# Polysketch attention into a squared-ReLU MLP: key and query projections in 64-row tiles, gated products on GpSimd, and a new order of the work

## The chip, the cores and the metric

The kernel runs on one core of a Trainium2 chip. The metric is the time of one execution on the device in microseconds. Of the kernel before there are three timed runs, 113.18, 113.51 and 114.02 us, with a median of 113.51, and one execution that was taken by the profiler, 113.43 us. The engines are called by the names of the profile: PE (matrix products), ACT (ScalarE), DVE (VectorE), POOL (GpSimd) and SP, which here only issues transfers.

## The reference

There are four batches of four heads, 1088 tokens each, head width 32, and two sketch matrices S1 and S2 of 8 x 32.

```python
def phi(x):
    a = np.einsum('rd,bhsd->bhsr', S1, x)
    b = np.einsum('rd,bhsd->bhsr', S2, x)
    return np.einsum('bhsi,bhsj->bhsij', a, b).reshape(*x.shape[:-1], r * r)
q_p, k_p = phi(q), phi(k)
kv = np.einsum('bhsf,bhsd->bhfd', k_p, v)
z = np.sum(k_p, axis=2)
num = np.einsum('bhsf,bhfd->bhsd', q_p, kv)
den = np.einsum('bhsf,bhf->bhs', q_p, z)[..., None] + 1e-06
attn = num / den
x = attn.transpose(0, 2, 1, 3).reshape(4352, 128)
h = np.maximum(x @ w_in, 0.0)          # w_in 128 x 2048
out = (h * h) @ w_out                  # w_out 2048 x 128
```

So every token of every head gets 64 features, the products of 8 values a with 8 values b. kv and z are sums over all tokens of a batch, so nothing of a batch's queries can be finished before all of its keys have been seen.

## The kernel before

**The plan.** The kernel does not issue its work as it describes it. Each step is recorded with `op(...)` (line 44): its engine or engines to choose from, an assumed duration, and the tiles that it reads and writes. `ORDER` (line 122) is a list of the numbers of all steps; `Plan.run` (line 67) walks through it, gives each PSUM tile a buffer, and the instructions are issued in that order, each on its engine. `ALT` names the steps that take the second of their engines. Each engine works through its own instructions in this order. A step whose `port` is true is one that the plan does not let run on DVE and GpSimd at the same time.

**PSUM.** There are two buffers `h` of two banks each and four buffers `t` of one bank each.

**Keys.** Batch 0 has code of its own (`k1`, line 357). For batches 1 to 3 `k_stage` (line 454) transposes the keys on DVE (`kT`, line 457), projects them (K1, line 463, eight matmuls of 128 rows by 32 columns into one t buffer, four for a and four for b), transposes the result to `kab` (line 468), does the same for the remainder of 64 tokens (K1r, line 476, and `kabr`, line 481), and multiplies a by b to `kp` on GpSimd (lines 488 and 495). `z_stage` sums for the denominator (z, line 406; Wc, line 415), `kv_stage` accumulates kv (line 426), and KV4T (line 448) transposes it.

**Queries.** For batches 1 to 3 `compact` (line 673) projects the transposed queries to a and b (qpr, line 686, eight matmuls into one t buffer) and to c, the denominator's part (qpc, four more). DVE transposes these (`qab`, line 690; `qc`, line 692), multiplies c by a into `t9` (ac, line 694), sums it (den), takes the reciprocal, scales a by it (`qaq`, a', line 698), and makes the products of a' and b in two halves (`qo`, line 706), each of which it transposes to `qd` (line 643). All the factors lie in SBUF. `x_turned` (line 648) multiplies qd by kv on 16 places of the array at once (line 662, rows and columns in groups of 32) into one h and two t buffers; it is called xe1, xe2 and xe3 for the batches 1 to 3, x1 and x8 for what remains. Its results are copied to `xT`.

**The MLP.** `f_stage` (line 740) takes 512 tokens (chunks 1 to 7) or 256 (0a, 0b and 8). F1 (line 764) writes two matmuls of 512 columns into an h buffer, ACT takes the ReLU into `r` (line 775), DVE or in places ACT squares it into `g` (line 784), and F2 (lines 791 and 794) accumulates into a t buffer, whose result goes through `osb` to the output by transfers that SP issues. F1 and the ReLU take turns on the two h buffers.

**Loads.** The keys and queries of batch 0 and most of its values come in by SP's queue. All later ones, `w_in` and `w_out` are issued by GpSimd, between its products. `load_v` (line 278) makes four transfers for a batch.

Of the kernel before, what the change touches and what calls it, by code (L numbers as in the profile page):

```python
# [17 lines left out]
class Op:  # L18
    __slots__ = ("eng", "fn", "name", "preds", "dma", "allocs", "uses", "n", "start", "end", "pri", "port")
# [11 lines left out]
class Plan:  # L31
# [12 lines left out]
    def op(self, eng, dur, fn, reads=(), writes=(), name="", dma=None, pri=None, port=False):  # L44
# [18 lines left out]
        o.n, o.start = len(self.ops), None  # L63
# [3 lines left out]
    def run(self, slots, t0=0.7):  # L67
        free = {e: t0 for e in ("PE", "ACT", "DVE", "POOL", "SP")}
        port = 0.0
# [9 lines left out]
        for o in self.order:  # L79
# [9 lines left out]
            if o.port and e in ("DVE", "POOL"):  # L89
                s = max(s, port)  # L90
            if o.dma is not None:
                l = lane["SW" if e == "POOL" else "HW"]
                s = max(s, l[-8] if len(l) > 7 else 0.0)
            o.eng, o.start, o.end = [(e, d)], s, s + d
            free[e] = s + d - (OVER.get(e, 0.0) if o.dma is None else 0.0)
            if o.port and e in ("DVE", "POOL"):
                port = s + d
# [16 lines left out]
TOK = ("0a", "0b", "7", "8")  # L114
SQA = ("0a", "0b", "1")
KPP = 5
FIRST4 = True
# [29 lines left out]
]  # L147
ALT = {67: 1, 91: 1, 110: 1, 127: 1, 131: 1, 137: 1, 155: 1, 161: 1, 318: 1, 387: 1, 423: 1, 425: 1}
# [3 lines left out]
def kernel(  # L152
# [39 lines left out]
    Wab = T("Wab", [128, 2, H, r])  # L192
    Wt = [T(f"Wt{b}", [128, 3, 32]) for b in range(B)]
# [13 lines left out]
    kab = ring("kab", 2, [128, 2, 8, 32])  # L207
    kabr = ring("kabr", 2, [64, 2, 32])
# [9 lines left out]
    qab = ring("qab", 1, [128, 2, 256])  # L218
    qc = ring("qc", 1, [128, 256])
# [7 lines left out]
    rr = ring("r", 3, [128, 4, 512], BF16)  # L227
    gg = ring("g", 3, [128, 4, 512], BF16)
    osb = ring("osb", 2, [128, 512])
    P = Plan()  # L230
    op, tmp = P.op, P.tmp

    def pb(t):
        return tb[t.i] if t.kind == "t" else hb[t.i][:, 0]
# [712 lines left out]
```

## Time and profile before

| what | value |
|---|---|
| median of three runs | 113.51 us |
| profiled execution | 113.43 us, its span 111.7 us, granted clock 0.99 |
| first F1 matmul | at 17.14 us |
| last F2 matmul ends | at 107.1 us |
| ACT, ReLU of 1024 columns | x67, 65.8 us, 1027 ns each |
| DVE, square of 2048 columns | x30, 35.9 us, 1201 ns each |
| DVE, qo of 1024 columns | x6, 9.9 us, 1651 ns each |
| GpSimd, kp of 512 columns | x12, 14.7 us, 1236 ns each |
| PE, F1 with 512 columns | x112, 389 ns each |

The profile shows one execution. Its span runs from the first instruction of the program to the last; the time of the execution is 1.7 us longer. Durations of single instructions include some overlap with the next one on the same engine, so that a piece of the chain, which goes from start to start, is shorter than the instruction's duration. A float32 matmul appears as two records.

### The profile page before, as it was taken

How to read it: one execution, taken by the hardware profiler on the slowest of the kernel's cores; microseconds unless marked ns; L12 is line 12 of the kernel's file. 1: busy time of each engine (PE TensorE's matmuls, PEld its weight loads, DVE VectorE, ACT ScalarE, POOL GpSimd, SP SyncE). 2: the span in 40 equal slices, each digit the busy share in tenths (PEclk: the TensorE clock that was granted, in tenths of full speed). 3: DMA queues.
4: the chain of work that ended last, by engine and by line, in shares of the span. 5: the costliest groups of instructions: out<-in, count | busy, mean ns of one | idle time of the engine just before them, and what ended most of it. 6: DMA issues, size and time to landing. Idle time of an engine off the chain costs nothing.

```text
span 111.7 us, 3330 instructions
## 1 busy us (share of the span) xinstructions
PE 102.7 (92%) x1388; PEld 63.4 (57%) x1388; DVE 92.7 (83%) x134; ACT 83.8 (75%) x113; POOL 32.9 (29%) x50
## 2 busy tenths in 40 slices
PE   7999999999997999979999999999799989999930
PEld 5677856767773645534455455445355545578910
DVE  2569699998999999999989997979877998675810
ACT  3240276999999479994789698969869998999910
POOL 7269147969999910720000000000000000000000
PEclk9999999999999999999999999999999999999995
DMA  1999999821880712000210220033003203222022
GB/s 38 286 262 244 211 387 260 230 79 61 257 246 3 214 55 61 16 6 12 35 18 6 41 47 6 10 61 58 6 0 59 35 5 56 39 47 50 6 70 71
DMA packets 18479, 10.20 MB, mean 91 GB/s; under 512 B 13936, under 2 KB 16928, under 8 KB 18464
## 3 DMA queue, kind: packets, MB, share of 16 engines
q0 software_dynamic: 1824, 6.11, 19.5%
q1 hardware_dynamic: 16384, 3.67, 15.8%
q10 hardware_dynamic: 256, 0.20, 0.8%
q8 instruction: 11, 0.18, 0.7%
q14 instruction: 4, 0.03, 0.1%
HBM read 8.80 MB, written 2.23 MB: 99 GB/s over the span
## 4 chain that ended last, share of the span: by engine, by line
PE 57%; DVE 19%; ACT 8%; issue 6%; DMA 4%; SPq 1%; DVEq 0%; ACTq 0%
PE h L764 20%; PE t L791 14%; ACT r L775 7%; DVE g L784 4%; PE t L426 4%; DMA kin<-in_k_dram 4%; PE t L794 3%; PE h L662 3%; DVE qo L706 3%; PE t L686 2%; DVE qd L643 2%; DVE qaq L698 2%; PE t L463 2%; PE t L540 2%; DVE qab L690 1%
## 5 line engine op out<-in xcount | busy, mean ns | idle before, releaser
L775 ACT ACTIVATE r<-h 128x1024 bf16<-128x1024 f32 x67 | 65.8, 1027 | 9.4 <-PE h L764 8.0
L784 DVE TENSOR_TENSOR g<-r 128x2048 bf16<-128x2048 bf16 x30 | 35.9, 1201 | 4.9 <-ACT r L775 4.9
L764 PE MATMUL h<-xT,w_in 128*128 128x512 bf16 (+1 forms) x128 | 36.1, 374 | 0.5 <-ACT r L775 0.4
L764 PEld LDWEIGHTS <-w_in 128*128 128x128 bf16 x160 | 19.5, 147 | 10.7 <-issue 3.4
L791 PE MATMUL t<-g,w_out 128*128 128x512 bf16 x96 | 24.7, 379 | 1.0 <-DVE g L784 1.0
L791 PEld LDWEIGHTS <-w_out 128*128 128x128 bf16 x96 | 9.1, 98 | 11.3 <-DVE g L784 1.5
L488 POOL TENSOR_TENSOR kp<-kab 128x512 f32<-128x512 f32 x12 | 14.7, 1236 | 1.8 <-DVE kab L468 1.8
L794 PE MATMUL t<-w_out,g 128*128 128x128 bf16 x160 | 10.7, 219 | 0.1
L794 PEld LDWEIGHTS <-g 128*128 128x128 bf16 x160 | 9.4, 98 | 1.9 <-issue 0.4
L706 DVE TENSOR_TENSOR qo<-qaq,qab 128x1024 f32<-128x1024 f32 x6 | 9.9, 1651 | 0.1
L643 DVE STREAM_TRANSPOSE qd<-qo 128x1024 f32<-128x1024 f32 (+1 forms) x8 | 9.2, 1158 | 0.1
L426 PEld LDWEIGHTS t<-kp,vin 128*32 128x32 f32 (+1 forms) x288 | 5.0, 108 | 5.7 <-issue 5.0
L426 PE MATMUL t<-kp,vin 128*32 128x64 f32 (+1 forms) x288 | 8.1, 225 | 0.0
L259 POOL DMA_DIRECT2D vin<-in_v_dram x14 | 7.8, 563 | 0.0
L662 PE MATMUL h<-qd,KV 32*32 32x256 f32 (+2 forms) x160 | 6.1, 331 | 0.9 <-ACT r L775 0.6
L912 PE MATMUL t<-const-bfloat16-1.0 128*128 128x256 bf16 x29 | 5.8, 339 | 0.8 <-PEq L931 0.8
L662 PE MATMUL t<-qd,KV 32*32 32x256 f32 (+2 forms) x160 | 6.3, 332 | 0.0
L784 ACT ACTIVATE g<-r 128x2048 bf16<-128x2048 bf16 x3 | 5.7, 1913 | 0.0
L686 PE MATMUL t<-qT,Wt 128*32 128x256 f32 x72 | 4.9, 385 | 0.8 <-DVE qT L515 0.8
L662 PEld LDWEIGHTS h<-qd,KV 32*32 32x32 f32 x160 | 3.4, 103 | 3.4 <-ACT r L775 1.8
L811 DVE STREAM_TRANSPOSE osb<-t 128x512 f32<-128x512 f32 x6 | 4.2, 693 | 1.0 <-PE t L791 1.0
L764 PE MATMUL h<-x,w_in 128*128 128x256 bf16 x32 | 4.9, 280 | 0.0
(118 smaller groups left out, 107.5 us busy)
## 6 DMA issues: line engine op xcount, KB each, us to landing
kin<-in_k_dram POOLq DMA_DIRECT2D x3, 544.0 KB, 6.4
qin<-in_q_dram POOLq DMA_DIRECT2D x3, 544.0 KB, 4.9
out_dram<-osb SPq DMA_DIRECT2D x44, 32.0 KB
vin<-in_v_dram POOLq DMA_DIRECT2D x6, 144.0 KB, 3.0
vin<-in_v_dram POOLq DMA_DIRECT2D x6, 128.0 KB, 4.8
kin<-in_k_dram SPq DMA_DIRECT2D x2, 256.0 KB
w_in<-in_moe_w_in_dram POOLq DMA_DIRECT2D x1, 512.0 KB, 6.2
w_out<-in_moe_w_out_dram POOLq DMA_DIRECT2D x1, 512.0 KB, 9.0
```

The costliest lines, as they stand in the source:

```text
L259: op(eng, 0.5 if eng != "POOL" else 0.8, lambda e: qs[eng].dma_start(out=o, in_=i), reads, writes, name, dma=kb / RATE, pri=(seq[0] - 200. ...
L426: pe.matmul(pb(tv)[32 * h : 32 * h + 32, :64], V[:Pn, h, m, :], kp_[:Pn, m, h].rearrange("p i j -> p (i j)"), start=(m == 0), stop=(m == 8 ...
L488: (pool if e == "POOL" else dve).tensor_tensor(out=kp_[:, 2 * u : 2 * u + 2].rearrange("p m h i j -> p (m h) i j"), in0=x, in1=y, op=ALU.mult)
L643: op("DVE", DVT(256 * G), lambda e: dve.transpose(qd_[:, g0 : g0 + G].rearrange("p g f t -> p (g f t)"), qo_[:, :G].rearrange("p g h x y - ...
L662: pe.matmul(bank[32 * h : 32 * h + 32, :n], KV4[rg if b is None else b][rows, y, 32 * h : 32 * h + 32], qd_[rows, :G, 2 * h + y, :], start ...
L686: pe.matmul(pb(t)[32 * c : 32 * c + 32, 256 * k_ : 256 * k_ + 256], Wt[b][:, f], qv[:, c], start=True, stop=True)
L706: dve.tensor_tensor(out=qo_.rearrange("p g h i j -> p (g h) i j"), in0=x_, in1=y_, op=ALU.mult)
L764: pe.matmul(hv()[:, x], w_inv[:, ct], X, start=True, stop=True)
L775: op("ACT", ACT(1024), lambda e, hv=hv, Rv=Rv, own=own: act.activation(Rv[:, own], hv(), ACTF.Relu), [th], [f"{Rk}.{u}"], f"relu {nm}.{g}")
L784: lambda e, R=R, G=G: dve.tensor_mul(G, R, R) if e == "DVE" else act.activation(G, R, ACTF.Square),
L791: pe.matmul(tb[to.i][:, :N], w_out[:, ct], Gv[:, y], start=(ct == 0), stop=(ct == CT - 1), skip_group_check=True)
L794: pe.matmul(tb[to.i][:, 128 * tt : 128 * tt + 128], Gv[:, y, tt * 128 : tt * 128 + 128], w_out[:, ct], start=(ct == 0 and tt == 0), stop=( ...
```

## The change

1. `W4` holds the sketch weights of a and b for two heads, so that 64 rows of keys or queries times 32 columns give a and b at once. K1 (with the remainder in it) and the a, b projection of the queries become matmuls of 64 rows by 32 columns, two row groups by four column groups, into the two banks of an h buffer. `kabr` and its K1r are gone; the transpositions to `kab` and to `qaf` (which replaces `qab`) sort a and b apart. The c projection stays on 128 rows.
2. qc is transposed within PSUM, and ac reads it there. a' is made in two halves. The first is written to PSUM and used from there for the first qo on DVE. The second half and its qo may be made by GpSimd; `ALT` gives the a' to it in all three batches and the qo has GpSimd as its first choice.
3. Every product on GpSimd that is a port step waits, by an added dependency, for the last port step that DVE has before it in the order. The plan's own account of such steps is finer.
4. The values of batches 2 and 3 are loaded through SP's queue. The fourth value load of batch 0, on ACT's queue, waits for the first load of keys.
5. Chunk 0a accumulates F2 with `w_out` held in the array and is transposed on its way out; the last 64 tokens of all batches (chunk 8) get `compact_rest`, which projects and transposes as the others do. The ReLU of chunks 5 to 8 may run on DVE (`RELUD`; three do). The squares of chunk 2 may run on ACT.
6. `ORDER` and `ALT` are new. `r` and `g` have buffers of twice the size, of which half is used, as `WIDE` is empty. Three copies of the weights on ACT are no longer made.

```diff
             if o.port and e in ("DVE", "POOL"):
-                s = max(s, port)
+                other = held["DVE" if e == "POOL" else "POOL"][-14:]
+                if e == "POOL" and held["DVE"]:
+                    s = max(s, held["DVE"][-1][1] + HOP)
...
-TOK = ("0a", "0b", "7", "8")
-SQA = ("0a", "0b", "1")
+TOK = ("0b", "7", "8")
+SQA = ("0a", "0b", "1", "2")
 KPP = 5
+WIDE = ()
+RELUD = ("5", "6", "7", "8")
...
-                 [f"{key}.{j4}"] + ([f"{key}.r{j4}"] if n == 9 else []), ["gate"] if b else [], first=True if b == 0 else False)
+                 [f"{key}.{j4}"] + ([f"{key}.r{j4}"] if n == 9 else []), ["gate"] if b else [f"{K0k}.0"] if j4 == 3 else [], first=b == 0)
+            if b == 0 and j4 == 3:
+                l.behind = P.w[f"{K0k}.0"]
...
-    for b in range(B):
+    op("POOL", 0.25, lambda e: pool.tensor_tensor(
+        out=W4.rearrange("p (a h i) -> p a h i", a=2, i=r), in0=Wab[:, :, :2], in1=Wab[:, :, 2:], op=ALU.add), ["Wab"], ["W4"], "W4")
+    for b in range(1):
         op("ACT", 0.22, lambda e, b=b: act.copy(Wt[b][:, :2], Wab.rearrange("p a h i -> p a (h i)")), ["Wab"], [f"Wt{b}.ab"], f"Wt{b}")
...
-        t = tmp()
+        th = tmp("h")
 
         def mm(e):
-            for a in range(2):
-                for j4 in range(4):
-                    pe.matmul(pb(t)[32 * j4 : 32 * j4 + 32, a * 256 : a * 256 + 256], W2[:, a],
-                              kt[:, JK[j4] * 32 : JK[j4] * 32 + 256], start=True, stop=True)
+            for j4 in range(4):
+                n = 288 if j4 < 3 else 256
+                for rw in range(2):
+                    rows_ = slice(64 * rw, 64 * rw + 64)
+                    pe.matmul(hb[th.i][32 * j4 : 32 * j4 + 32, rw, :n], W4[rows_], kt[rows_, JK[j4] * 32 : JK[j4] * 32 + n], start=True, stop=True)
+            for rw in range(2):
+                rows_ = slice(64 * rw, 64 * rw + 64)
+                pe.matmul(hb[th.i][96:, rw, 256:288], W4[rows_], kt[rows_, :32], start=True, stop=True)
...
+        op("DVE", DVT(576), lambda e: dve.transpose(
+            kb_.rearrange("p a m (rw x) -> p rw m a x", rw=2), hb[th.i][:, :, :288].rearrange("p rw (m a x) -> p rw m a x", a=2, x=16)),
+           [th], [kbk], f"kab{b}")
...
+        t1, t3, th = tmp(), tmp(), tmp("h")
+
+        def mm_ab(e):
+            for c in range(4):
+                for rw in range(2):
+                    rows_ = slice(64 * rw, 64 * rw + 64)
+                    pe.matmul(hb[th.i][32 * c : 32 * c + 32, rw, :256], W4[rows_], qv[rows_, c], start=True, stop=True)
...
+        op("DVE", DVT(512), lambda e: dve.transpose(
+            qa_.rearrange("p a (g rw x) -> p rw g a x", rw=2, x=16), hb[th.i][:, :, :256].rearrange("p rw (g a x) -> p rw g a x", a=2, x=16)),
+           [th], [qak], f"qa{nm}")
+        op("PE", 0.46, mm_c, ks_ + [f"Wt{b}.c"], [t1], f"qpc{nm}")
+        op("DVE", DVT(256), lambda e: dve.transpose(pb(t3)[:, :256], pb(t1)[:, :256]), [t1], [t3], f"qc{nm}")
...
+            def scaled(u=u):
+                return qq[:, :16] if u else pb(t3)[:, 256:384].rearrange("p (g i) -> p g i", i=r)
+
+            def fa(e, us=us, scaled=scaled):
+                return (pool if e == "POOL" else dve).tensor_tensor(
+                    out=scaled(), in0=av[:, us], in1=dn[:, us, None].to_broadcast([128, 16, r]), op=ALU.mult)
...
-            op("DVE", DVE(1024), fn, [qqk, abk], [f"{qok}.0", f"{qok}.2"], f"qo{nm}.{u}", port=True)
+            op([("POOL", 2.13), ("DVE", DVE(1024))] if u else "DVE", DVE(1024), fn, [qak, qqk if u else t3], [f"{qok}.0", f"{qok}.2"],
+               f"qo{nm}.{u}", port=u == 1)
...
+                op([("ACT", ACT(1024))] + [("DVE", 0.17 + 1024 * 0.00105)] * (nm in RELUD), 0,
+                   lambda e, hv=hv, Rv=Rv, own=own: act.activation(Rv[:, own], hv(), ACTF.Relu) if e == "ACT"
+                   else dve.tensor_scalar_max(Rv[:, own], hv(), 0.0),
...
-            load_v(b, "POOL")
+            load_v(b, "POOL" if b == 1 else "SP")
...
-            o.fn(e)
+            o.ins = getattr(o.fn(e), "ins", None)
+            if o.port and e == "DVE":
+                turn = o.ins
+            elif o.port and e == "POOL" and turn is not None:
+                tc.add_manual_dep(o.ins, turn.name, SYNC, reason="one of the two at a time")
```

More of the change, by code (lines that the diff above doesn't have):

```diff
@@ L18 @@
 class Op:
-    __slots__ = ("eng", "fn", "name", "preds", "dma", "allocs", "uses", "n", "start", "end", "pri", "port")
+    __slots__ = ("eng", "fn", "name", "preds", "dma", "allocs", "uses", "n", "start", "end", "pri", "port", "behind", "ins")
 class Tmp:
@@ L62, in op @@
         o.preds = list(dict.fromkeys(preds))
-        o.n, o.start = len(self.ops), None
+        o.n, o.start, o.behind, o.ins = len(self.ops), None, None, None
         self.ops.append(o)
@@ L68, in run @@
         free = {e: t0 for e in ("PE", "ACT", "DVE", "POOL", "SP")}
-        port = 0.0
+        held = {"DVE": [], "POOL": []}
         dmat = {}
@@ L89, in run @@
             if o.port and e in ("DVE", "POOL"):
-                s = max(s, port)
+                other = held["DVE" if e == "POOL" else "POOL"][-14:]
+                if e == "POOL" and held["DVE"]:
+                    s = max(s, held["DVE"][-1][1] + HOP)
+                near = 0.06 if e == "DVE" else 0.0
+                while any(a <= s + near and s < b - 1e-9 for a, b in other):
+                    s = next(b for a, b in other if a <= s + near and s < b - 1e-9)
+                held[e].append((s, s + d))
             if o.dma is not None:
@@ L93, in run @@
                 s = max(s, l[-8] if len(l) > 7 else 0.0)
+                if e == "POOL":
+                    held[e].append((s, s + 0.75 * d))
             o.eng, o.start, o.end = [(e, d)], s, s + d
             free[e] = s + d - (OVER.get(e, 0.0) if o.dma is None else 0.0)
-            if o.port and e in ("DVE", "POOL"):
-                port = s + d
             if o.dma is not None:
@@ L258, in load @@
         seq[0] += 1
[L259 to L260 removed]
+        return op(eng, 0.5 if eng != "POOL" else 0.8, lambda e: qs[eng].dma_start(out=o, in_=i), reads, writes, name,
+           dma=kb / (RATE if first else 285.0), pri=(seq[0] - 200.0 if first is True else first) if first else None)
     def rows(x, b):
@@ L677, in compact @@
         qv = qt.rearrange("p (g c t) -> p c g t", c=4, t=32)
+        ks_ = [f"{qtk}.{x}" for x in range(3)]
         i_ = ntok[0]
         ntok[0] += 1
-        (ab, abk), (c_, ck), (t9_, t9k), (dn, dnk), (qq, qqk) = qab(0), qc(0), t9(i_), den(i_), qaq(i_)
-        t1, t2 = tmp(), tmp()
-        def mm(e, t, fs):
-            for k_, f in enumerate(fs):
-                for c in range(4):
-                    pe.matmul(pb(t)[32 * c : 32 * c + 32, 256 * k_ : 256 * k_ + 256], Wt[b][:, f], qv[:, c], start=True, stop=True)
@@ L694, in compact @@
-        op("DVE", DVE(256), lambda e: dve.tensor_tensor(out=t9_[:, :, :r], in0=c_.rearrange("p (g i) -> p g i", i=r), in1=av, op=ALU.mult),
-           [ck, abk], [t9k], f"ac{nm}", port=True)
+        (qa_, qak), (t9_, t9k), (dn, dnk), (qq, qqk) = qaf(0), t9(i_), den(i_), qaq(i_)
+        t1, t3, th = tmp(), tmp(), tmp("h")
[4 more added lines that the diff above has]
+                    pe.matmul(hb[th.i][32 * c : 32 * c + 32, rw, :256], W4[rows_], qv[rows_, c], start=True, stop=True)
@@ new lines, in mm_c @@
+        def mm_c(e):
+            for c in range(4):
+                pe.matmul(pb(t1)[32 * c : 32 * c + 32, :256], Wt[b][:, 2], qv[:, c], start=True, stop=True)
+        op("PE", 0.50, mm_ab, ks_ + ["W4"], [th], f"qpr{nm}")
+        op("DVE", DVT(512), lambda e: dve.transpose(
+            qa_.rearrange("p a (g rw x) -> p rw g a x", rw=2, x=16), hb[th.i][:, :, :256].rearrange("p rw (g a x) -> p rw g a x", a=2, x=16)),
+           [th], [qak], f"qa{nm}")
+        op("PE", 0.46, mm_c, ks_ + [f"Wt{b}.c"], [t1], f"qpc{nm}")
@@ L781, in f_stage @@
                        [f"{Rk}.{u}"], [f"{Gk}.{u}"], f"sq {nm}.{g}", port=True)
-            if not split:
+            if wide and y4:
+                op("DVE", 0.17 + 4096 * 0.00052, lambda e, R=R8, G=G8: dve.tensor_mul(G, R, R),
+                   [f"{Rk}.{x}" for x in range(4)], [f"{Gk}.{x}" for x in range(4)], f"sq {nm}.{g2}", port=True)
+            elif not split and not wide:
                 op([("DVE", 0.17 + 2048 * 0.00052)] + [("ACT", ACT(2048))] * (nm in SQA), 0,
@@ L915 @@
                 tick = FILL
-            o.fn(e)
+            o.ins = getattr(o.fn(e), "ins", None)
[3 more added lines that the diff above has]
+                tc.add_manual_dep(o.ins, turn.name, SYNC, reason="one of the two at a time")
+            if o.behind is not None:
+                tc.add_manual_dep(o.ins, o.behind.ins.name, SYNC, reason="order of the first loads")
 _INS = ['q', 'k', 'v', 'S1', 'S2', 'moe_w_in', 'moe_w_out']
```

129 lines of the change are left out of this document (71 added, 58 removed), and 46 rows, old and new, of the table ORDER.

## The prediction

> **What bounds the kernel now.** I read the totals of the page first, then busy time by stage, then the chain of waits, then the timeline where DVE and GpSimd meet. The totals name no single bound:
>
> ```profile
> PE 102.7 (92%) x1388; PEld 63.4 (57%) x1388; DVE 92.7 (83%) x134; ACT 83.8 (75%) x113; POOL 32.9 (29%) x50
> ```
>
> So I cut the span at the first F1 matmul (17.14 us) and at the starts of the three large products with qd (xe1, xe2, xe3: 39.45, 60.90, 79.60), up to the last F2 (107.1), and call the parts A, B, C, D; what lies before is the head.
>
> ```profile
> 17.14:39.45 22.31, 21.51 (x384) 14.37 (x385) 21.57 (x32) 19.66 (x22) 20.48 (x25) 1.00 0.58 165
> 39.45:60.90 21.45, 20.44 (x259) 10.53 (x260) 20.99 (x26) 17.71 (x23) 2.80 (x4) 1.00 0.11 26
> 60.90:79.60 18.70, 18.12 (x222) 9.07 (x220) 17.29 (x21) 15.79 (x20) 0.00 (x0) 1.00 0.20 34
> 79.60:107.10 27.50, 26.60 (x314) 17.51 (x314) 21.21 (x27) 24.19 (x31) 0.00 (x0) 1.00 0.19 32
> ```
>
> Columns: length, then busy PE, PEld, DVE, ACT, POOL. Three engines are near full in each part, so an edit pays only if the fullest engine of its part loses work. Busy PE hides waits, so I price by the chain's pieces, which run from start to start:
>
> ```profile
> 15.46 0.56 PE h L524 x8
> 16.03 1.00 PE t L463 x16
> 17.03 0.11 PE t L476 x8
> ...
> 59.91 1.00 PE t L686 x16
> ...
> 73.31 0.58 PE h L764 x2
> ...
> 75.59 0.43 PE h L764 x2
> 76.03 0.86 PE t L791 x4
> ...
> 89.21 2.86 ACT r L775 x3
> ```
>
> An F1 pair costs 0.43, four F2 matmuls 0.86, eight projection matmuls (16 records) 1.00. The same pieces give 0.36 for 16 records of kv, 1.3 for an xe (of the 1.43 from 60.91 to 62.34, with short gaps in it), and on DVE 1.13 for a square or a 1024-wide transposition, 0.6 for a 512-wide one. On ACT a relu costs 0.92 (three in a row last 2.85, one 1.02) and a square 1.9. At 89.21 ACT and not PE is last. Sums of these over the work of each part, in the order that each kernel gives it, before:
>
> A: PE 19.4, DVE 19.1, ACT 19.3. B: 18.7, 17.0, 16.5. C: 16.6, 16.8, 14.1. D: 24.9, 20.7, 24.1. The parts lasted 2.9, 2.8, 1.9 and 2.6 more than their fullest engine. In A and B much of that is here:
>
> ```profile
> 7.68 1.09 POOL L382 TENSOR_TENSOR kp<-kabz 128x512 f32<-128x512 f32 x1
> 8.03 0.69 DVE L382 TENSOR_TENSOR kp<-kabz,t 128x512 f32<-128x512 f32 x1
> ...
> 24.04 1.18 DVE L784 TENSOR_TENSOR g<-r 128x2048 bf16<-128x2048 bf16 x1
> 24.20 1.96 POOL L488 TENSOR_TENSOR kp<-kab 128x512 f32<-128x512 f32 x1 [0.98 <-DVE kab L468]
> ...
> 45.74 3.59 DVE L706 TENSOR_TENSOR qo<-qaq,qab 128x1024 f32<-128x1024 f32 x1
> 46.16 2.09 POOL L488 TENSOR_TENSOR kp<-kab 128x512 f32<-128x512 f32 x2
> ```
>
> A DVE product of two SBUF tiles and a GpSimd product exclude each other: qo took 3.59 where its undisturbed fellows took 1.18, and kp waited out the square (1.96 for 1.06). A DVE product with one input in PSUM (tile t, 8.03) ran at 0.69 beside GpSimd. DVE lost 2.41 at 45.74, 1.65 in the qaq at 29.60 (2.03 for 0.38) and 0.35 each in t at 26.85 and qo at 31.66: 4.8 in all.
>
> **The change, part by part.**
>
> *64-row tiles.* K1 and the a,b projection become eight matmuls on eight places of the array instead of two turns on four. That row groups run side by side I take from the xe: 64 records on 16 places in 1.3, against 16 records on 4 places in 1.00. The nearest row of the same tile (64*32, L524) is 0.56 for eight records. So 0.5 instead of 1.0, and K1 with its remainder 0.6 instead of 1.11: 0.5 less six times, one in the head, three in A, two in B. Bounds: nothing (groups take turns) to 0.5. An F1 pair after a visit to another shape costs 0.58 instead of 0.43. One such visit goes (K1r of the last batch, alone between F1 pairs): -0.15, left out. Inside a visit the shape now changes from the a,b to the c projection, three times, which no row here shows. The Trainium skill (TensorEngine Tiling (Array Packing), Key Properties) says that a change of tiling mode, as against a change of tile, drains the TensorE; by it these three would cost a step each, 0.45 at the trace's 0.15, and the sum below would be 109.6 instead of 109.2.
>
> *DVE.* Off it: three 1024-wide products (3 x 1.13, to GpSimd), half of each a' (3 x 0.2), three kabr transpositions (0.4), and most of the 4.8 of stalls, since ac and qo.0 now read one input from PSUM like the product at 8.03. Onto it: three relus of 1024 (3.4, priced as the 1024-wide transposition), nine hundred more copied columns and two small transpositions of chunk 8 (1.2), osb0a and osb0b (0.7). The new transpositions write 16-wide pieces; kT in four-dimensional form took 0.44 for 256 columns, as the plain one did, so I price them at width. Twice that, the upper bound, puts 1.9 on DVE in A, where ACT still equals it, and 1.2 in B: +0.6.
>
> *ACT.* Off it in D: five relus, two now on DVE, the others done earlier in the order (the third DVE relu is in C). Onto it: in A two relus drawn forward and qp0.1 (0.5), in B a square. Three W copies (0.25 each) and osb0a, osb0b (0.37 each) leave it.
>
> *GpSimd.* Its products grow by 3 x (2.1 + 0.45), two kp of 1.03 being 2.1 for 1024, and a' of 128 columns lying under the 0.64 of a 256-wide kp; eight v issues leave (8 x 0.57 = 4.5, from the page's 7.8 for 14). Each product waits for DVE's latest two-SBUF product. Behind it on its queue stand further kp, the q load of the last batch, and qo.1, for which qd.1 on DVE waits, and then the xe. Before it ended at 49.3; kv of the last batch was wanted at 65, so a delay of kp alone costs nothing; one of qo.1 or q does.
>
> *v on SP.* SP held nine first loads and then output stores; of the eight v loads of batches 2 and 3, three now stand ahead of the first store and five among the first four. Each waits for the kv stage two batches before, and the stores queue behind it. v of batch 2 was wanted at 52, and a store's tile only at the second chunk after: I take nothing, and at most one landing, 3.0. The fourth v load of batch 0 waits on ACT for the first k load, in by 3.97; ACT's next copy came at 5.95 and v was wanted at 9.22: nothing.
>
> *Head.* qoT0.1 (0.44) moves behind the first F1, K1 loses 0.5, KV4T (0.22) moves ahead: -0.7; F1 at 16.4. xT0.0, which it needs, ended at 16.6 behind the same qoT0.1, so it follows.
>
> The same sums after: A: PE 19.0, DVE 19.6, ACT 21.3. B: 17.7, 17.1, 17.0. C: 17.0, 16.4, 14.3. D: 23.5, 20.2, 19.4. Three of them in full: ACT in A is 16 relus 14.7, three squares 5.4, qp0.1 0.5 and small copies 0.7. PE in B is 15 F1 pairs 6.5, seven F2 fours 6.0, an xe 1.3, kv 1.7, two a,b and two c projections 2.0, KV4T 0.2. DVE in B is five squares 5.6, two qo 2.3, two qd 2.3, qT 1.1, two qa 1.2, two each of qc, ac, den, reciprocal and a' 3.0, two output transpositions 1.2, a copy 0.3. The remaining loss is my choice: A is ACT's, which has its own queue, 1.3; B 2.0, C 1.8, D 1.9 (D's ACT no longer competes). So A 22.6 (+0.3), B 19.7 (-1.8), C 18.8 (+0.1), D 25.4 (-2.1), head -0.7: -4.2. The profiled execution took 113.43 (span 111.7 and 1.7 around it), 0.08 under the median 113.51. 113.4 - 4.2 = 109.2.
>
> **Rivals.**
>
> *Tighter still (106.2).* If each part loses 1.0 over its fullest engine, the parts are 22.3, 18.7, 18.0, 24.5: -6.5, with the head -7.2. For it: the stalls were most of the loss in A and B. Against: C and D had none and lost 1.9 and 2.6.
>
> *The h buffers (111.7).* K1 and the a,b projection leave t (four buffers) for h (two), which F1 and relu take turns on. With one h, a relu comes every 0.43 + 1.02 = 1.45 instead of 0.92. An h is held for 0.5 of matmul, up to 1.2 of DVE's current work and 0.7 of transposition, so a holding costs up to 0.9; three in A, where ACT is fullest, and two in B: five at 0.5 are 2.5. For it: at 77.36 and 89.21 ACT is already last. Against: at every holding ACT has squares or copies too. The Trainium skill (TensorEngine Tiling, PSUM Bottleneck) says that tiling does not speed up the evacuation of PSUM, which can become the bottleneck; no run here shows it yet.
>
> *The tiles do not run together (110.7).* Then 0.5 in the head and 1.0 in B are not won; A is ACT's anyway. L524 and L662 speak against it.
>
> *Slower: DVE and GpSimd in lockstep (115.9).* The gate and the port make one queue of both engines' two-SBUF products. Where GpSimd is late, DVE's next square waits for a whole product, in B behind kp3.6, a'e2.1, qoe2.1, kp3.2, qoe3.1: 1.03 + 0.45 + 2.13 + 1.03 + 2.13 = 6.8; in A behind kp2.4, a'e1.1 and one late qoe1.1: 3.6. DVE's work is then 23.2 in A and 23.9 in B; with 0.9 and 1.0 of other waits the parts are 24.1 and 24.9, 1.5 and 5.2 over the forecast's: 109.2 + 6.7 = 115.9. It decides from some 4.2 of stalls that reach the end. For it: 3.59 at 45.74. Against: DVE's order puts five undisturbed transpositions and copies beside qoe1.1, and the gate lets waiting squares through first.
>
> **How the numbers follow.** Forecast 0.52 (its own range 107.3 to 111), tighter 0.12, h 0.15, tiles apart 0.08, lockstep 0.13. The range 106.0 to 112.8 leaves out lockstep and the edges. One per cent of 113.5, about what can be told from no change, is 1.1. Faster: 0.52 + 0.12 + 0.11 of h + 0.06 of tiles apart = 0.81; slower: 0.11 of lockstep; the rest, 0.08, within.
>
> **What would show it.** K1 and the a,b projection at 0.5 to 0.6 in the chain; F1 first at 16.4; qo on DVE at 1.2 throughout; xe1 at 39.0, xe2 at 58.7; ACT no longer last at the end. Wrong would be: squares of 2 us and more beside qo on GpSimd, or ACT waiting for F1 after each kab and qa.

## The result, and the profile after

The changed kernel takes 108.58 us, the median of four runs (108.07 to 109.34), beside 113.56 (113.18 to 114.02) for the kernel before on the same chip: a ratio of 0.9565, with a 95% interval from 0.9496 to 0.9634. Faster, by 4.4% with 3.7 to 5.0 as bounds. The profiled execution took 108.07, its span 106.3, at a granted clock of 1.00. In some executions either kernel is some per cent slower than in the rest; the ratios leave those out, while the median times given with the experiments include them.

The totals and the shares of the chain of waits, on the page of the changed kernel:

```profile
PE 98.3 (92%) x1356; PEld 62.3 (59%) x1369; DVE 88.6 (83%) x138; ACT 80.0 (75%) x101; POOL 33.6 (32%) x49
PE 78%; ACT 11%; issue 4%; DVE 1%; DVEq 0%; ACTq 0%
```

The same shares of the chain, on the page of the kernel before:

```profile
PE 57%; DVE 19%; ACT 8%; issue 6%; DMA 4%; SPq 1%; DVEq 0%; ACTq 0%
```

The shares of busy time have hardly moved: that of PE is 92% as before. The chain tells more: DVE had 19% of it and is now off it almost wholly.

The same four stretches as in the prediction, A to D, in the view of busy time by window (length, then busy PE, PEld, DVE, ACT, POOL):

```profile
16.07:37.87 21.80, 21.02 (x372) 14.98 (x375) 20.11 (x33) 20.57 (x23) 14.69 (x17) 1.00 0.63 156
37.87:57.15 19.28, 18.92 (x247) 9.59 (x255) 18.14 (x26) 17.41 (x21) 7.03 (x7) 1.00 0.15 40
57.15:75.49 18.34, 18.10 (x211) 9.54 (x221) 16.70 (x21) 15.41 (x16) 1.93 (x2) 1.00 0.15 25
75.49:101.05 25.56, 24.92 (x327) 16.78 (x330) 22.61 (x31) 21.02 (x25) 0.00 (x0) 1.00 0.26 43
```

Cut at the first record of each marker, which can be compared across kernels to some hundredths, the parts are:

| | head | A | B | C | D | rest |
|---|---|---|---|---|---|---|
| before | 17.07 | 22.38 | 21.39 | 18.78 | 27.46 | 4.57 |
| forecast | 16.4 | 22.6 | 19.7 | 18.8 | 25.4 | 4.6 |
| after | 16.00 | 21.87 | 19.23 | 18.32 | 25.60 | 5.29 |

The pieces of the chain that the prediction named, first from the whole chain, then from the chain followed back in 36 to 52 us:

```profile
15.41 0.61 PE h L480 x7
16.07 0.60 PE h L822 x4
18.20 2.76 ACT r L834 x3
...
32.07 0.61 PE h L480 x7
...
87.76 1.04 ACT r L834
...
89.96 1.24 DVE r L835
```

```profile
39.36 0.59 PE h L698 x16
39.95 0.57 PE t L702 x8
40.52 0.37 PE h L822
```

K1 (L480) takes 0.66 with its remainder (15.41 to 16.07) and the a, b projection (L698) 0.59, where the kernel before had 1.00 for each (1.11 with K1's remainder). F1 follows the c projection (L702) at once. At the end, one ReLU on ACT (87.76) and one on DVE (89.96) are still last now and then, where ACT held the chain for 2.86 in one piece before.

The groups by line, operation and shape (busy, mean ns, then idle time before and what ended it):

```profile
L496 POOL TENSOR_TENSOR kp<-kab 128x512 f32<-128x512 f32 x12 | 12.6, 1069 | 11.9 <-DVE g L847 10.1 <-DVE kab L488 1.8
L731 POOL TENSOR_TENSOR qo<-qaq,qaf 128x1024 f32<-128x1024 f32 x3 | 5.9, 1955 | 4.1 <-DVE g L847 3.1 <-DVE t L723 0.9
L731 DVE TENSOR_TENSOR qo<-t,qaf 128x1024 f32<-128x1024 f32 x3 | 3.6, 1205 | 0.0
L488 DVE STREAM_TRANSPOSE kab<-h 128x576 f32<-128x576 f32 x3 | 2.3, 775 | 0.5 <-PE h L483 0.4
L705 DVE STREAM_TRANSPOSE qaf<-h 128x512 f32<-128x512 f32 x3 | 2.1, 717 | 0.7 <-PE h L698 0.6
```

The mean of kp is back at 1069 ns from 1236, and that of qo on DVE at 1205 from 1651. GpSimd now waits 13.2 us for squares on DVE (10.1 and 3.1), which is the gate at work. No instruction on DVE took over 1.3 us; before, a qaq took 2.03 and two of the qo 1.53 and 3.59. How the two engines meet, in the timeline around 46 us (start, duration):

```profile
46.04 1.95 POOL L731 TENSOR_TENSOR qo<-qaq,qaf 128x1024 f32<-128x1024 f32 x1 [0.95 <-DVE t L723]
...
46.42 1.19 DVE L731 TENSOR_TENSOR qo<-t,qaf 128x1024 f32<-128x1024 f32 x1
```

Both products run at their own pace side by side: the one on DVE reads tile `t` in PSUM.

### The profile page after: what moved, and what is told of

Read it like the earlier page. It is cut to its first block, busy times and chain, and to the rows that moved or that the text cites. A ratio compares the mean times of both kernels' runs of the same rounds, so it can differ in the third digit from the quotient of the medians.

```text
span 106.3 us, 3296 instructions
## 1 busy us (share of the span) xinstructions
PE 98.3 (92%) x1356; PEld 62.3 (59%) x1369; DVE 88.6 (83%) x138; ACT 80.0 (75%) x101; POOL 33.6 (32%) x49
## 3 DMA queue, kind: packets, MB, share of 16 engines
q0 software_dynamic: 1440, 5.00, 17.2%
## 4 chain that ended last, share of the span: by engine, by line
PE 78%; ACT 11%; issue 4%; DVE 1%; DVEq 0%; ACTq 0%
PE h L822 25%; PE t L854 18%; ACT r L834 8%; PE t L857 8%; PE t L441 6%; PE t L977 5%; PE h L670 3%; ACT g L847 2%; PE t L548 2%; DVE r L835 1%; PE h L480 1%; PE h L698 1%; PE t L702 1%; PE t L670 1%; PE t L379 1%
## 5 line engine op out<-in xcount | busy, mean ns | idle before, releaser
L834 ACT ACTIVATE r<-h 128x1024 bf16<-128x1024 f32 x64 | 62.4, 1027 | 8.6 <-PE h L822 6.7
L822 PE MATMUL h<-xT,w_in 128*128 128x512 bf16 (+1 forms) x120 | 34.0, 373 | 0.5
L854 PE MATMUL t<-g,w_out 128*128 128x512 bf16 (+1 forms) x107 | 26.3, 363 | 0.3
L496 POOL TENSOR_TENSOR kp<-kab 128x512 f32<-128x512 f32 x12 | 12.6, 1069 | 11.9 <-DVE g L847 10.1
L857 PE MATMUL t<-w_out,g 128*128 128x128 bf16 x128 | 8.5, 219 | 0.0
L857 PEld LDWEIGHTS <-g 128*128 128x128 bf16 x128 | 7.6, 98 | 1.0 <-DVE g L830 0.2
L731 POOL TENSOR_TENSOR qo<-qaq,qaf 128x1024 f32<-128x1024 f32 x3 | 5.9, 1955 | 4.1 <-DVE g L847 3.1
L977 PEld LDWEIGHTS <-const-bfloat16-1.0 128*128 128x128 bf16 x30 | 3.6, 127 | 2.1 <-issue 0.9
L876 DVE STREAM_TRANSPOSE osb<-t 128x512 f32<-128x512 f32 (+1 forms) x7 | 4.5, 660 | 0.0
L835 DVE TENSOR_SCALAR r<-h 128x1024 bf16<-128x1024 f32 x3 | 3.7, 1222 | 0.6 <-ACT r L834 0.4
(129 smaller groups left out, 109.6 us busy)
```

The costliest lines, as they stand in the source:

```text
L496: return (pool if e == "POOL" else dve).tensor_tensor(out=kp_[:, 2 * u : 2 * u + 2].rearrange("p m h i j -> p (m h) i j"), in0=x, in1=y, o ...
L731: return (pool if e == "POOL" else dve).tensor_tensor(out=qo_.rearrange("p g h i j -> p (g h) i j"), in0=x_, in1=y_, op=ALU.mult)
L822: pe.matmul(hv()[:, x], w_inv[:, ct], X, start=True, stop=True)
L834: lambda e, hv=hv, Rv=Rv, own=own: act.activation(Rv[:, own], hv(), ACTF.Relu) if e == "ACT"
L835: else dve.tensor_scalar_max(Rv[:, own], hv(), 0.0),
L854: pe.matmul(tb[to.i][:, :N], w_out[:, ct], Gv[:, y], start=(ct == 0), stop=(ct == CT - 1), skip_group_check=True)
```

## Experiments

All ratios are to the kernel before on the same chip, with 95% intervals. Parts are those of the table above, from one profiled execution each, and a difference in brackets is to the changed kernel's row unless it is said otherwise. All kernels but one are edits of the changed kernel.

**The changed kernel again.** No edit.

> The changed kernel again, as the measure for the runs beside it: 0.957 of the time of before, with an interval narrower than the first one's.

Measured: 109.32 us, 0.9583 [0.9539, 0.9628]. The profiled execution has head 17.16, then A 21.86, B 19.24, C 18.31, D 25.60: the four parts repeat within 0.01, the head does not. The trace ties the head to the first loads: from the first z matmul of batch 0 to the first F1 it is 8.50 in both executions, and 8.84 in the kernel before. So of the 1.07 by which the two profiled heads differ, 0.34 belongs to the change. The parts are therefore compared singly; the totals of two profiled executions cannot be, to better than about 1 us. The parts are not free of chance either: in the run with the ReLUs on ACT, below, A is 0.54 longer though nothing of A was edited. And the ratios of the runs without the gate, with a' in SBUF, with the ReLUs on ACT and with v through GpSimd have intervals that overlap with this one, so what is said of those four rests on a part of one execution and on the instructions that its timeline shows.

**The gate alone, on the kernel before** (with the products returning their instruction).

```diff
-            o.fn(e)
+            ins = getattr(o.fn(e), "ins", None)
+            if o.port and e == "DVE":
+                turn = ins
+            elif o.port and e == "POOL" and turn is not None:
+                tc.add_manual_dep(ins, turn.name, SYNC, reason="one of the two at a time")
```

> The kernel before with the added dependency alone: each GpSimd product waits for the last two-SBUF step that DVE has before it in the order. My theory: the qo of 3.59 us goes back to 1.2, since the kp that held it now waits for DVE, and part B falls from 21.4 by 1 to 2 us; the qaq of 2.0 in part A stays, since its kp stands ahead of it in the order; in all 0.983 to 0.99 of before. Rival, the stall was hidden behind PE or the wait moves to kp: 0.995 to 1.005, B unchanged.

Measured: 111.15, 0.9773 [0.9739, 0.9808]; against the kernel before A 21.43 (-0.95), B 20.22 (-1.17), C and D the same. More than expected. The timeline of this kernel where the kernel before had its qo of 3.59:

```profile
44.69 1.22 DVE L706 TENSOR_TENSOR qo<-qaq,qab 128x1024 f32<-128x1024 f32 x1
...
47.71 0.62 POOL L495 TENSOR_TENSOR kp<-kabr 64x256 f32<-64x256 f32 x1 [7.97 <-DVE g L784]
```

qo is at 1.22, and GpSimd's last kp waits 7.97 for its turn without anybody missing it. In A the slow qaq and qo are gone too. This one dependency, alone, gains 2.3%, about half of what the whole change does.

**The changed kernel without the gate.**

```diff
-                tc.add_manual_dep(o.ins, turn.name, SYNC, reason="one of the two at a time")
+                pass
```

> The changed kernel without the added dependency of GpSimd's products on DVE's; the data's own dependencies stay. My theory: GpSimd's 13 us of waiting for squares go, its products start earlier, run beside DVE's squares and hold them up to 2 us in several places: +1 to +2 us, 0.966 to 0.975, and squares on DVE of 1.5 us and more appear in A and B. Rival, the gate is itself a cost because qo of the second half and the last batch's q load come later: 0 to -1 us, 0.948 to 0.957.

Measured: 109.27, 0.9628 [0.959, 0.9665]; A 21.98 (+0.11), B 19.64 (+0.41). The timeline has the loss, a square beside a kp:

```profile
31.58 1.07 POOL L496 TENSOR_TENSOR kp<-kab 128x512 f32<-128x512 f32 x1
31.71 2.02 DVE L847 TENSOR_TENSOR g<-r 128x2048 bf16<-128x2048 bf16 x1 [0.70 <-ACT r L834]
```

An a' took 1.64 for 0.27 at 46.48 as well, and two others 0.50 for 0.29. DVE thus stands still for 2.6 here, against 4.8 in the kernel before. The gate is worth 0.5 in these parts, a quarter of what it is worth in the old order. The products in PSUM, the three moved to GpSimd and the new order have taken the other collisions away or hidden them; which of them did was not told apart.

**128 rows again.** The weights of a row group stand in a matrix with zeros for the other group's rows, and every matmul runs over all 128 rows. Outputs, buffers and transpositions stay; `W4` is filled by a copy instead of a sum.

```diff
-    W4 = T("W4", [128, 32])
+    W4 = T("W4", [128, 2, 32])
...
-                    pe.matmul(hb[th.i][32 * j4 : 32 * j4 + 32, rw, :n], W4[rows_], kt[rows_, JK[j4] * 32 : JK[j4] * 32 + n], start=True, stop=True)
+                    pe.matmul(hb[th.i][32 * j4 : 32 * j4 + 32, rw, :n], W4[:, rw], kt[:, JK[j4] * 32 : JK[j4] * 32 + n], start=True, stop=True)
...
-                    pe.matmul(hb[th.i][32 * c : 32 * c + 32, rw, :256], W4[rows_], qv[rows_, c], start=True, stop=True)
+                    pe.matmul(hb[th.i][32 * c : 32 * c + 32, rw, :256], W4[:, rw], qv[:, c], start=True, stop=True)
```

> The changed kernel with the 64-row tiles alone undone: the same eight matmuls into the same h buffer, in the same order, but over all 128 rows, so that the two row groups take turns on each column group. My theory (row groups run side by side in the changed kernel, part A is ACT's): the K1 and a,b pieces go from 0.6 to 1.1, which costs 0.5 in the head, at most 0.5 in A and 1.0 in B, about +1.5 us over the changed kernel, 0.970 of before. Rival 1, the tiles take turns already: the pieces stay at 0.6 and the time does not move. Rival 2, all PE time counts: +3.0 us, 0.983.

Measured: 110.92, 0.9771 [0.9732, 0.981]; A 22.89 (+1.02), B 19.87 (+0.64), and 8.99 for 8.50 in the stretch of the head before F1. The chain of this kernel, from 15 to 36 us:

```profile
15.65 1.05 PE h L480 x10
...
22.45 0.90 PE h L698 x16
23.35 0.91 PE h L480 x11
```

A record of the same 256 columns lasts 384 to 389 ns in either form, so a single matmul is no quicker on 64 rows; two row groups at a time are. The visits take 0.9 to 1.09 for 0.59 to 0.61. The tiles are worth 2.1, of which half lies in A, where the prediction had counted nothing.

**The three products of GpSimd back on DVE.** The numbers name steps that take their second engine: each of the three edits gives a' its first, DVE, and the qo behind it its second, DVE too.

```diff
-    89: 1, 108: 1, 114: 1, 128: 1, 129: 1, 130: 1, 137: 1, 157: 1, 178: 1, 185: 1, 242: 1, 278: 1, 297: 1, 314: 1,
-    315: 1, 387: 1, 389: 1, 402: 1, 419: 1, 420: 1, 422: 1, 452: 1, 466: 1, 501: 1,
+    89: 1, 108: 1, 114: 1, 128: 1, 129: 1, 130: 1, 137: 1, 157: 1, 179: 1, 185: 1, 242: 1, 278: 1, 298: 1, 314: 1,
+    315: 1, 387: 1, 389: 1, 403: 1, 419: 1, 420: 1, 422: 1, 452: 1, 466: 1, 501: 1,
```

> The changed kernel with the second half of a' and its qo back on DVE in all three batches, everything else and the order kept. DVE gets 1.3 us more work three times. My theory (B is near DVE's and PE's limit, A is ACT's): +0.5 in A and +2 in B and C, about 0.978 of before, with no stalls beside kp because the gate orders them. Rival, it was the end of the stalls and not the work taken off DVE that won the time: within 0.5 us of the changed kernel, 0.957 to 0.962.

Measured: 109.6, 0.9667 [0.9631, 0.9704]; A +0.57, B +0.51, C +0.23. That is 1.3 for some 4 us of work put back on DVE: about half of what was expected reaches the end. Not all of A's 0.57 belongs to the edit: counted from the first F1, the ReLU that starts at 27.38 in the changed kernel comes 0.14 late already, before the first of the moved products runs.

**The first a' in SBUF instead of PSUM.**

```diff
-                return qq[:, :16] if u else pb(t3)[:, 256:384].rearrange("p (g i) -> p g i", i=r)
+                return qq[:, 16 - 16 * u : 32 - 16 * u]
```

> The changed kernel with the first half of a' written to SBUF and read from there, so that the first qo of each batch has two SBUF inputs; order, gate and the rest kept. My theory (a DVE product with one input in PSUM runs beside GpSimd, one with two in SBUF does not): where qo.0 meets qo.1 on GpSimd, in the batches 2 and 3, it takes 2.3 to 2.9 us instead of 1.2, and part B gets 1 to 2 us longer than 19.2. Rival, a DVE stall there is hidden: the same long qo, but B at 19.2 to 19.5. A third way, no exclusion: qo stays at 1.2.

Measured: 110.26 (108.95 to 110.5), 0.9666 [0.9598, 0.9734]; B 19.48 (+0.25), the other parts within 0.07. The timeline of this kernel on both engines, at the two places where their qo meet:

```profile
46.31 1.95 POOL L731 TENSOR_TENSOR qo<-qaq,qaf 128x1024 f32<-128x1024 f32 x1 [0.93 <-DVE qaq L723]
46.72 2.63 DVE L731 TENSOR_TENSOR qo<-qaq,qaf 128x1024 f32<-128x1024 f32 x1
...
56.59 1.95 POOL L731 TENSOR_TENSOR qo<-qaq,qaf 128x1024 f32<-128x1024 f32 x1
57.42 2.21 DVE L731 TENSOR_TENSOR qo<-qaq,qaf 128x1024 f32<-128x1024 f32 x1
```

The same instruction took 1.19 and 1.21 at these places with its input in PSUM. Each now ends 1.1 after the one on GpSimd does, which is about a whole undisturbed product: it stood still until the other was through. The Trainium skill (GPSIMD Engine Reference, Specifications) says that GpSimd shares its SBUF interfaces with VectorE and that they contend when a DVE instruction has two SBUF inputs; these rows agree, and add that one input in PSUM is enough to be free of it. The two stalls sum to 2.4, yet only 0.25 shows in a part.

**Three ReLUs back on ACT** (of chunks 5 to 8).

```diff
-    315: 1, 387: 1, 389: 1, 402: 1, 419: 1, 420: 1, 422: 1, 452: 1, 466: 1, 501: 1,
+    315: 1, 387: 1, 389: 1, 402: 1, 419: 1, 420: 1, 466: 1,
```

> The changed kernel with the three relus that DVE makes in chunks 5, 6 and 7 back on ACT. My theory (ACT was last at several places of D before): C +0.3, D +1.0 over 18.3 and 25.6, because PE waits where ACT has three relus in a row. Rival, D is PE's own time now, whoever makes the relus: D within 0.3 of 25.6.

Measured: 110.04, 0.9649 [0.9596, 0.9702]; C +0.17, D +0.30. Three ReLUs off ACT are worth 0.5. D is 25.90 without them and was 27.46 before, so most of its gain is something else. A grew by 0.54, though nothing of A was edited. The chain of this kernel from 22 to 25 us has 0.3 of it:

```profile
22.67 0.88 PE h L698 x12
23.55 0.06 PE h L480 x4
23.60 0.16 PE h L698 x4
23.76 0.45 PE h L480 x10
```

Here the row groups ran apart: one group's last four a, b records stand behind K1's first of the other group. From the first a, b record to F2 it is 1.59, and 1.29 in the repeated run, with the same instructions in the same order up to there. Why the group started late in this execution was not found. With the products back on DVE the same stretch took 1.36, with four records of one group late.

**One square of A from ACT to DVE** (chunk 0a).

```diff
-    89: 1, 108: 1, 114: 1, 128: 1, 129: 1, 130: 1, 137: 1, 157: 1, 178: 1, 185: 1, 242: 1, 278: 1, 297: 1, 314: 1,
+    89: 1, 114: 1, 128: 1, 129: 1, 130: 1, 137: 1, 157: 1, 178: 1, 185: 1, 242: 1, 278: 1, 297: 1, 314: 1,
```

> The changed kernel with the first square of chunk 0a on DVE instead of ACT. By sums ACT then has 19.5 in part A and DVE 20.7. My theory (A is ACT's): A falls from 21.9 by 0.5 to 1.0. Rival, DVE or PE is as near to the limit in A as ACT: A stays or gets longer by up to 1.

Measured: 112.24, 0.9871 [0.9834, 0.9908]; A 24.39 (+2.52), the rest unchanged. The timeline of this kernel in A:

```profile
25.61 1.03 PE L854 MATMUL t<-g,w_out 128*128 128x256 bf16 x8 [1.83 <-DVE g L847]
25.64 0.62 POOL L503 TENSOR_TENSOR kp<-kab 64x256 f32<-64x256 f32 x1 [5.52 <-DVE g L847]
...
26.88 3.12 POOL L496 TENSOR_TENSOR kp<-kab 128x512 f32<-128x512 f32 x3
...
29.96 0.62 POOL L503 TENSOR_TENSOR kp<-kab 64x256 f32<-64x256 f32 x1
30.01 3.71 DVE L847 TENSOR_TENSOR g<-r 128x2048 bf16<-128x2048 bf16 x1
30.55 1.06 POOL L496 TENSOR_TENSOR kp<-kab 128x512 f32<-128x512 f32 x1
```

The expectation was that 1.9 less on ACT shortens A. Instead F2 of chunk 0a waited 1.83 for the square in DVE's queue, the gate held GpSimd for 5.52 behind that square, and GpSimd's products, now late, ran into the next square, which took 3.71. This is the lockstep rival, at one place and at 2.5 us. The run shows that DVE's time counts in A; what 1.9 less on ACT would give without the square on DVE, it does not show.

**v through GpSimd again.**

```diff
-            load_v(b, "POOL" if b == 1 else "SP")
+            load_v(b, "POOL")
```

> The changed kernel with the eight v loads of batches 2 and 3 issued by GpSimd again, at the same places of the order. GpSimd gets 8 x 0.57 us more issuing, three of them before the first kp of batch 2, and the loads of batch 3 wait on its queue for kv of batch 1 (at 31). My theory (as predicted, SP costs nothing and GpSimd has slack in A): qo on GpSimd in A about 1 us later, xe1 behind it, A +0.5 to +1 over 21.9, B within 0.5 of 19.2. Rival, GpSimd has no slack in A: everything behind the loads comes 3 us or more later, A +2 and more. Third, nothing moves: 0.958.

Measured: 108.99, 0.9636 [0.9594, 0.9678]; B +0.33, A unmoved. Each issue takes GpSimd 0.57; a kp came late enough at 38.41 to meet a square, which took 2.09. The v on SP is worth 0.3, in B and not in A.

**The projections of batch 3 in two t buffers instead of an h.** For the other batches no t buffers are free in this order.

```diff
+KT2, QT2 = (3,), (3,)
...
-        th = tmp("h")
+        th = [tmp(), tmp()] if b in KT2 else [tmp("h")]
...
-        t1, t3, th = tmp(), tmp(), tmp("h")
+        t1, t3, th = tmp(), tmp(), [tmp(), tmp()] if b in QT2 else [tmp("h")]
```

> The changed kernel with K1 and the a,b projection of batch 3 alone in two t buffers instead of an h buffer (two transpositions of half the width each for it); for the other batches no t buffers are free. My theory (ACT has squares to do whenever an h is held): A and B within 0.3 us of 21.9 and 19.2. Rival, the h rival of the prediction: each of the two holdings costs some 0.5, so A and B fall by about 0.5 each.

Measured: 109.95, 0.9678 [0.9636, 0.972]; B 19.94 (+0.71), the other parts within 0.01. The first of the two holdings lies in A: giving its h back changes nothing there. The second lies in B, where the timeline of this run has a new wait:

```profile
50.92 1.02 PE L861 MATMUL t<-g,w_out 128*128 128x512 bf16 x4 [0.65 <-DVE qaf L711]
```

F2 waits 0.65 for DVE to empty a t buffer. So B shows what a t buffer costs there, and not what an h is worth. The timeline of the changed kernel shows what ACT does while these two h are held, from the start of their transposition at 32.93 and at 49.38, and at the third place, behind the a, b projection of batch 2:

```profile
31.78 1.90 ACT L847 ACTIVATE g<-r 128x2048 bf16<-128x2048 bf16 x1
32.93 0.78 DVE L488 STREAM_TRANSPOSE kab<-h 128x576 f32<-128x576 f32 x1 [0.40 <-PE h L483]
...
41.14 1.94 ACT L834 ACTIVATE r<-h 128x1024 bf16<-128x1024 f32 x2 [0.67 <-PE t L702]
...
48.99 1.90 ACT L847 ACTIVATE g<-r 128x2048 bf16<-128x2048 bf16 x1
49.38 0.72 DVE L705 STREAM_TRANSPOSE qaf<-h 128x512 f32<-128x512 f32 x1
```

At the two places of batch 3 it is at a square and needs no h; so it is in batch 1, at squares from 20.99 to 24.70. At 41.14 it has waited 0.67 for F1, which came behind the c projection; how much of that an h more would save was not run. The Trainium skill (TensorEngine Tiling (Array Packing), PSUM Bottleneck) warns that evacuation can become the limit once the array is faster; no run here shows that it did.

**Two stores of chunk 7 issued by GpSimd.**

```diff
-                    load("SP", f"st o{nm}.{x}", o[j], osv[:, x], 128, [], [ok])
+                    load("POOL" if nm == "7" and x % 2 else "SP", f"st o{nm}.{x}", o[j], osv[:, x], 128, [], [ok])
```

> The changed kernel with two of the four stores of chunk 7 issued by GpSimd, which is idle then. In the changed kernel SP issues them 0.58 us apart and the last store only 1.0 us after the last F2; it was 0.56 before. My theory (the 5.3 us from the last F2 to the end of the span are longer than before's 4.6 because SP's issues queue up): the end falls to 4.6 to 4.8, -0.6 us, 0.952 to 0.955 of before. Rival, the landing of the last transfer decides and not its issue: 5.2 to 5.4 as it is. A third way: GpSimd's transfers land later and the end gets longer.

Measured: 109.84, 0.9608 [0.9565, 0.9652]; A to D within 0.01 and the rest 5.29 as before. (The head of its profiled execution was disturbed and is not compared.) So SP's queue at the end costs nothing. The last two stores are issued together there, one of them, of 64 KB, on ACT's queue, 0.4 after the last copy's start.

**Three parts undone together**: 128 rows, the products on DVE, no gate; the edits are those above.

> The changed kernel with three parts undone at once: projections over 128 rows, the second a' and qo on DVE, no gate. What is left of the change is the order, the PSUM inputs, v on SP, relus on DVE, chunks 0a and 8. If the parts add up as single undoings did (1.0 + 0.6 + 0.1 in A, 0.6 + 0.5 + 0.4 in B, 0.2 in C, 0.5 in the head): about +4 us, 0.993 of before, so that the rest wins next to nothing by itself. Rival 1, they overlap (all three relieve the same DVE and PE waits): +2 to +3 us, 0.975 to 0.985. Rival 2, without the gate and with qo back on DVE the long stalls return: over 1.0, with a product of 2.5 us and more on DVE.

Measured: 113.15, 113.20, 114.92 and 115.13, median 114.06, beside 113.43, too scattered for an interval; the profiled execution is that of 113.15, with A 22.89, B 22.02, C 18.55, D 25.60. All of the gain is gone, though the new order, the ReLUs on DVE and v on SP are still in. A grew by 1.02, where the three single undoings sum to 1.70, and C by 0.23, as one of them did. B grew by 2.8, where they sum to 1.56. The timeline of B has a longer stall than any of the three had alone:

```profile
38.17 4.15 POOL L496 TENSOR_TENSOR kp<-kab 128x512 f32<-128x512 f32 x4
...
39.59 4.96 DVE L847 TENSOR_TENSOR g<-r 128x2048 bf16<-128x2048 bf16 x2
```

Four kp in a row, and a square that started at 39.59 took 3.82 of that 4.96: it got no turn until the whole run of products was over.

## Why the prediction held, and where it was off

The forecast was a gain of 4.2, to 109.2. By the ratios, 0.9565 and 0.9583, the gain is 4.7 to 4.9 of 113.5. The sum was 0.5 to 0.7 short of that, from errors of both signs.

*Right: the stalls.* The 4.8 us on DVE are gone, with the mechanism that was named, and undone one at a time (gate, PSUM, GpSimd's products) each brings its own slow instruction or lost time back. B was forecast at 19.7 and came to 19.2, xe2 at 57.1 for 58.7.

*Right: the tiles run together*, at 0.59 for the a, b projection and 0.66 for K1 with its remainder, where 0.5 and 0.6 were said. The rival of tiles apart falls as a rule; a group ran late in two of the runs, by 0.3 in that with the ReLUs on ACT and by 0.07 in that with the products back on DVE.

*The step that failed: "A is ACT's".* Its sum for ACT, 21.3, was too high, as the window has 20.57 busy in 21.80, and more than the size was wrong. With it three visits in A were counted at nothing; undone they cost 1.02, the difference between the forecast of +0.3 and the -0.5 that came, with 0.2 to spare. Moving a square of 1.9 from ACT to DVE made A longer by 2.5. In A the chain passes from PE to ACT (2.76 of ReLUs at 18.20) and back, so the fullest engine's sum was not the limit, and time on PE or DVE there was not free.

*The head* was forecast 0.7 shorter; the fixed part, from batch 0's first z matmul on, is 0.34 shorter. K1 gives 0.49 by itself, so the rest of the stretch grew. qoT0.1 (0.44) did leave it, but the first projection of queries, ahead of z before (0.39 at 7.80, L595), stands behind z now (0.59 at 8.01, L603), which the prediction had not listed. The 16.0 of the profiled execution owes the rest to when its first loads landed.

*C* was taken to grow by 0.1 and came 0.46 shorter. With GpSimd's product back on DVE it is 0.23 longer, with the ReLUs back on ACT 0.17.

*D* came at 25.6 for 25.4. Of its 1.86 the ReLUs are 0.3, where the forecast let ACT's relief carry more. The other 1.56 is in every variant, the one with three parts undone included. The order draws two F1 pairs and an F2 of four out of D, 1.7 by the prices of the prediction, and fits; the order was not undone alone, so this is argued and not shown. As moved work it need not be a gain by itself: the run with three parts undone has C and D shorter by 2.1 than the kernel before and is hardly faster, as B is longer by 0.6, A by 0.5 and the rest by 0.5.

*The rest* behind the last F2 was taken as unchanged and grew by 0.7. The last store is issued by SP, 0.56 behind the end of the last F2 in the kernel before (107.64) and 1.01 behind it in the changed one (102.03); from there to the end of the span it is 4.0 (111.66) and 4.3 (106.31). The issue does not decide it: with two stores taken off SP the last one is issued 0.44 behind F2, and the rest stays at 5.29. The twelve profiled executions in the new order have 4.8 to 5.9, the two in the old one 4.6 and 4.5, so it seems to go with the change and not with chance; what it is stays open.

*Small prices.* The new transpositions go by width (717 ns for 512 columns, 695 before; 775 for 576), so the doubling in the bounds falls. Products on GpSimd cost 1.96 and 0.41 for the estimated 2.1 and 0.45. v on SP was taken at nothing and is a gain of 0.3.

*The change of tiling mode* within a visit was weighed at 0.15, three times. It happens twice, as in batch 3 the c projection (46.81) and the a, b projection (48.55) stand apart. Its price can be read from what stands behind the a, b projection. In the timeline of the changed kernel K1 follows in the same form in batch 1, and the c projection in another form in batch 2:

```profile
21.66 0.66 PE L698 MATMUL h<-qT,W 64*32 64x256 f32 x16
22.16 0.71 PE L480 MATMUL h<-kT,W 64*32 64x288 f32 x16
...
39.29 0.66 PE L698 MATMUL h<-qT,W 64*32 64x256 f32 x16
39.88 0.64 PE L702 MATMUL t<-qT,Wt 128*32 128x256 f32 x8
```

In the run with 128 rows both projections have one form:

```profile
41.04 1.09 PE L698 MATMUL h<-qT,W 128*32 128x256 f32 x16
41.93 0.64 PE L702 MATMUL t<-qT,Wt 128*32 128x256 f32 x8
```

From start to start it is 0.50 without and 0.59 with the change of form. Over 128 rows four turns take 0.89, so two of them 0.45, which makes the price 0.14. So a change costs 0.09 to 0.14 here, near the 0.15 that the prediction left out of its sum. The Trainium skill (TensorEngine Tiling (Array Packing), Key Properties) has a drain at each change of mode; the trace agrees, with this size. The 109.6 was further from the time all the same, as other terms erred the other way.

*The h buffers*, the rival at 111.7, priced five holdings at 0.5 each. At four of them ACT is at squares, and at one it waits 0.67, behind the c projection. A and B came out shorter than forecast, so the 2.5 did not appear; whether a smaller cost is hidden there was not shown.

*Lockstep*, the rival on the other side, was priced at 6.7 and did not happen in the changed kernel: squares stayed below 1.32. But its mechanism is real and near. One square more on DVE in A brought it on at 2.5 and the v loads' issues on GpSimd in B at 0.3; with three parts undone, the gate among them, a run of four kp held a square for 2.6. *Tighter still* took a loss of 1.0 over the fullest engine's sum in each part. Over PE's sums of 17.7, 17.0 and 23.5 it was 1.5 in B, 1.3 in C and 2.1 in D, where the forecast had 2.0, 1.8 and 1.9: between the two in B and C, and beyond the forecast in D.

## What to carry to other kernels

Where two engines exclude each other, look for single instructions of two or three times their usual length in the timeline. One dependency that makes the engine with idle time wait can be worth more than moving work: 2.1 on the old order, where the three moved products are worth at most 1.3 in the new one. What such a remedy is worth depends on the others and on the order (the same dependency is worth 0.5 in the new one), so single gains need not add up: undone together, three parts cost less than their sum in A and more in B. Do not call a part bound by the engine with the largest sum while the chain in it changes hands: test each engine's time in it by an edit. In an order with little slack an instruction that moves can cost more than its own length, as the square of 1.9 did that cost 2.5.

## What the runs showed that was not expected

A square on DVE that starts during a run of GpSimd products waits for the run and not for one product: 3.82 beside a run of four kp, for the 1.2 that it takes alone; it ended 1.1 after the run did.

The gate's 2.3% on the old order (0.9773) came from a wait added to an engine which then idled 7.97 in one piece.

With 64-row tiles the two row groups need not keep step: the same instructions in the same order took 1.59 in one execution, 1.36 in another and 1.29 in the changed kernel's own.

Between executions of the changed kernel the first F1 came from 16.0 to 17.2 us with the landing of the first loads, while A to D repeated within 0.01; a third execution of the same A, in the run with the ReLUs on ACT, took 0.54 longer. Neither a total nor a part of one execution is proof without the instruction that explains it.
